# A PSUM tile for each of the seven products of a Strassen group

## Chip, core and metric

The kernel runs on one core of a Trainium2 chip. The metric is the time of one execution on the device in microseconds, 1038.79 as the median of three runs.

## What is computed

Four batches of eight heads attend over 576 positions of 64 elements: only scores within `tau` of a row's maximum count. The result, 2304 rows of 512, goes through four experts, weighted by the row's normalised domain probabilities.

```python
scores = scale * np.matmul(q, k.transpose(0, 1, 3, 2))
thresh = np.max(scores, axis=-1, keepdims=True) - tau
scores = np.where(scores >= thresh, scores, -1000000000.0)
scores = scores - np.max(scores, axis=-1, keepdims=True)
attn = np.exp(scores)
attn = attn / (np.sum(attn, axis=-1, keepdims=True) + 1e-09)
x = np.matmul(attn, v).transpose(0, 2, 1, 3).reshape(B * S, H * D)   # 2304 x 512
p = domain_probs / (domain_probs.sum(-1, keepdims=True) + 1e-09)
for e in range(E):                                                    # E = 4, F = 1024
    h = np.maximum(x @ w1[e], 0.0)
    out += p[:, e:e + 1] * (h @ w2[e])
```

## The kernel before

Every fp32 operand of a matmul of the experts is split into a high and a low fp16 half, and a product of two such operands is three matmuls. Experts 0 and 1 (`unit`, products at L1372, second layer at L1414) run between the steps of attention. Experts 2 and 3 (`unit7`, L1564) run after it and form their first layer by Strassen's scheme, seven products of half blocks in place of eight. The 2304 rows are dealt in five row sets (`GR`); a row set and an expert make a unit, ten units in all. Four sets have m = 256 columns, the set `(8,)` has m = 128.

A unit has four groups, k = 0 to 3, of seven products each. A product (`product`, six matmuls at L1627) sums into a PSUM region. Its readers bring it, scaled, into the SBUF tile `qt`: `copy` on ScalarE (L1657) for the first product of a group, `add` on VectorE (L1647) for the others; the product of S1 and T1 is added twice. `hidden` then makes a hidden block's high half on ScalarE (L1668) and its low half on VectorE (L1675). The second layer takes these in steps of three matmuls of 512 columns (`g2`, L1707), eight steps to a row tile, and `done` (L1725) adds the result to the accumulator. `run` (L1872) deals the steps of the unit before between the products of a unit.

PSUM holds eight banks of 512 fp32 columns. Attention has the pool `ma`, two tiles of a bank (`ET`, `rp` and `av` by use), and the tile `S` of three banks, taken once; the other three are the pool `mm` of the second layer. The Strassen products live in what is attention's: the first, third, fifth group of a unit's order and so on put their regions a, b, f, g at columns 0, 1280, 1024 and 256 of `S`; the groups between take `av` for a and g and `ET` for f and b. The seven products use a, b, f, g, a, b, g in this order. The maxima over the weight pairs (`w_pair`, L1451, with `all_max`) use spare columns of `S` (`am`, L350).

The order of all instructions comes from `Plan` (L22 to L216), a list scheduler: each operation has an engine, an estimated time, the values it reads and writes, the tiles of pools that it uses, and a priority. A tile can be had when a slot of its pool is free, and a slot is free `FREED` = 150 ns after the last user of the tile in it ends. The tiles of a pool are given in the order in which they are first named. The simulated order is then the order in which each engine's instructions are emitted, and the program's waits follow from who reads and writes which tile. Two things tie the stages: `later_kind` (L313) closes the pools of attention at the first tile of a later pool and opens those of `later` in their space, and `ends` holds every operation on a later pool's tile back until all of attention's products with v (`av_`) are done:

```python
ends = {i for i, o in enumerate(pl.ops) if o[2].__name__ == "av_"}
...
for o in pl.ops:
    if any(pl.kinds[x[0]][0] in later for x in o[4]):
        o[3].update(ends)
```

Of the kernel before, what the change touches and what calls it, by code (L numbers as in the profile page):

```python
# [9 lines left out]
FP32 = mybir.dt.float32  # L10
# [214 lines left out]
def topk_attention_moe_kernel(  # L225
# [43 lines left out]
    for name, n in (  # L269
# [3 lines left out]
        pools[name] = pool(name, n, on=first)  # L273
    pools["ma"] = pool("ma", 2, space=PSUM)

    s_all = pool("s", 1, space=PSUM).tile([128, 1536], FP32, name="S")
    pl.pool("b", 1)
# [32 lines left out]
    kind("acc2", "w", "w", [128, 2, DM], FP32)  # L310
    later = {"wp": 8, "xf": 1}

    def later_kind(name, p, shape, dt):  # L313
        def make():
            if p not in pools:
                first.close()
                for n, k in later.items():
                    pools[n] = ctx.enter_context(
                        tc.tile_pool(name=n, bufs=k, reuse_waits="tile")
                    )  # L320
            return pools[p].tile(shape, dt, tag=name, name=name)

        pl.kind(name, p, make)

    for name, n in later.items():
        pl.pool(name, n)
    later_kind("WP", "wp", [128, 2, 2816], FP16)
    later_kind("xf", "xf", [128, 4, 2, 256], FP32)
    kind("XT", "xt", "xt", [128, NK, 2, 128], FP16)
# [1121 lines left out]
    def w_pair(e, k, kd, prio):  # L1451
# [18 lines left out]
        )  # L1470
        au = am(("w", e, k))
        all_max(
# [88 lines left out]
    TX = {"T1": (0, 0), "T3": (0, 1), "T4": (1, 0), "T2": (1, 1)}  # L1561
    n_quad = 0

    def unit7(name, xs, m, tiles, u, last):  # L1564
        nonlocal n_quad
        e, top = PARTS[u][0], -1000.0
# [38 lines left out]
        for k in range(4):  # L1605
            P, qt, q = ("WP", (e, k)), ("qt", (u, name, k)), (u, name, k)
            if n_quad % 2:
                ps = [("av", ("q", q)), ("ET", ("q", q))]
                at = {"a": (0, 0), "g": (0, 256), "f": (1, 0), "b": (1, 256)}
            else:  # L1610
                ps = [("S", ("q", q))]
                at = {"a": (0, 0), "g": (0, 256), "f": (0, 1024), "b": (0, 1280)}
            n_quad += 1
            reg = lambda r, ps=ps, at=at: pl.t(*ps[at[r][0]])[:, at[r][1]:at[r][1] + m]
            pu = lambda r, ps=ps, at=at: ps[at[r][0]]
            wcs = wc[:, e, k:k + 1]
# [37 lines left out]
            def copy(reg=reg, pu=pu, qt=qt, q=q, tmp=tmp, wcs=wcs):  # L1654
                act(
                    m / 0.96 + 190,
                    lambda: nc.scalar.activation(  # L1657
                        out=tmp(0), in_=reg("a"), func=ACTF.Copy, scale=wcs
                    ),
                    [("p", "a") + q, ("wc", u)], [("t", 0) + q], use=[pu("a"), qt], prio=top,  # L1660
                )

            def hidden(i, j, f, qt=qt, q=q, tmp=tmp):
# [17 lines left out]

            first += [
                [(product, "a", "11", "11"), (copy,)],
                [(product, "b", "S2", "T2"), (add, "b", 0, 1)],
                [(product, "f", "S1", "T1"), (add, "f", 1, 2)],
                [(product, "g", "S3", "T3"), (add, "g", 1, 1), (add, "f", 1, 3),
                 (hidden, 3, 1, k + 4)],
                [(product, "a", "12", "21"), (add, "a", 0, 0), (hidden, 0, 0, k)],
                [(product, "b", "S4", "22"), (add, "b", 2, 2), (hidden, 2, 1, k)],
                [(product, "g", "22", "T4"), (add, "g", 1, 1), (hidden, 1, 0, k + 4)],  # L1690
            ]
# [80 lines left out]
    with tc.manual_schedule():  # L1772
# [59 lines left out]

        ends = {i for i, o in enumerate(pl.ops) if o[2].__name__ == "av_"}
        for u in range(NP1, len(PARTS)):
# [95 lines left out]
```

## Time and profile before

| | |
|---|---|
| runs | 1037.43, 1038.79, 1040.62 us (median 1038.79) |
| profiled execution | 1037.09 us, span 1035.3 us |
| TensorE busy | 978.8 us, 95% of the span |
| VectorE busy | 728.4 us, 70% |
| ScalarE busy | 558.8 us, 54% |
| GpSimd busy | 244.4 us, 24% |
| DMA | 95.99 MB, 93 GB/s on the mean |
| granted TensorE clock | 0.979 of full speed on the mean |

The engines are PE (TensorE; PEld is its weight load, which runs beside a matmul), DVE (VectorE), ACT (ScalarE), POOL (GpSimd) and SP (SyncE, which issues DMAs). Busy shares are averages over the whole span; attention and the experts 0 and 1 fill it up to about 664 us, the Strassen units the rest. A row of a timeline groups like instructions that follow each other: start, duration, engine, line, what is written and read, how many, and in brackets the idle time of the engine ahead of it and who ended it. The ends of matmuls are modelled, so a row's duration can reach past the next row's start.

### The profile page before, as it was taken

Reading aid. Unit: us, or ns where it says so; the run is one execution under the profiler, and the core shown is the slowest. Engines: PE = TensorE matmul, PEld = TensorE weight load, DVE = VectorE, ACT = ScalarE, POOL = GpSimd, SP = SyncE. Lnnn points to the kernel's source line nnn. Section 1 sums busy time; section 2 is a strip of 40 time slices with the busy share of each in tenths; the row PEclk is TensorE's granted clock in tenths of the full one; section 3 lists DMA queues with packets and bytes.
Section 4 is the critical chain, followed back from the end, with each engine's and each line's share of the span. In section 5 each row is a group of like instructions: output and inputs, shape, how many; then the busy total and the mean of one; then the engine's idle time right before and its main releaser. Section 6 shows DMA issues by size and latency. Waiting matters only on the chain.

```text
span 1035.3 us, 20228 instructions
## 1 busy us (share of the span) xinstructions
PE 978.8 (95%) x7538; PEld 626.3 (60%) x7538; DVE 728.4 (70%) x1788; ACT 558.8 (54%) x1177; POOL 244.4 (24%) x401
## 2 busy tenths in 40 slices
PE   6779978999989999999999999999999998999998
PEld 4465644666666556666556776766666666666663
DVE  3787778888778887888883636878665577655551
ACT  4788777766776768676765678533212132212120
POOL 1112526334344325433342323200000000000000
PEclk9889977999999999999999999999999999999999
DMA  6800477775689477865774224200200202001001
GB/s 173 246 11 12 101 159 172 127 129 96 145 148 215 89 120 154 157 139 107 134 114 100 82 95 141 82 21 22 72 31 22 72 11 72 11 1 52 31 1 41
DMA packets 243234, 95.99 MB, mean 93 GB/s; under 512 B 209600, under 2 KB 230080, under 8 KB 243136
## 3 DMA queue, kind: packets, MB, share of 16 engines
q1 hardware_dynamic: 243136, 94.71, 41.6%
q8 instruction: 59, 0.97, 0.4%
q14 instruction: 39, 0.32, 0.1%
HBM read 40.41 MB, written 14.16 MB: 53 GB/s over the span
## 4 chain that ended last, share of the span: by engine, by line
PE 76%; DMA 8%; DVE 6%; SPq 4%; ACT 3%; issue 2%; POOL 1%; DVEq 0%; ACTq 0%; POOLq 0%
PE mm L1707 16%; PE mm L1372 15%; PE mm L1414 15%; PE S L1627 9%; PE av L1256 5%; PE av L1627 4%; DMA PT<-E 4%; PE S L933 4%; PE ET L1627 3%; SPq L413 3%; DVE qt L1647 3%; DMA wraw<-in_moe_w_dram 2%; PE av L1265 1%; PE S L939 1%; DMA T<-R 1%
## 5 line engine op out<-in xcount | busy, mean ns | idle before, releaser
L1707 PE MATMUL mm<-WP,h 128*128 128x512 f16 x864 | 221.2, 379 | 0.0
L1414 PE MATMUL mm<-W,h 128*128 128x512 f16 x864 | 206.0, 380 | 0.7 <-ACT hr L1384 0.7
L1627 PEld LDWEIGHTS <-WP 128*128 128x128 f16 x1680 | 153.2, 97 | 86.0 <-issue 33.0
L1372 PEld LDWEIGHTS <-W 128*128 128x128 f16 x2016 | 175.6, 99 | 33.4 <-issue 5.2
L1372 PE MATMUL mm<-X,W 128*128 128x256 f16 (+1 forms) x1632 | 181.6, 268 | 4.7 <-ACT hr L1384 4.7
L1668 ACT ACTIVATE h<-qt 128x256 f16<-128x256 f32 (+1 forms) x160 | 61.8, 394 | 227.4 <-DVE qt L1647 227.3
L1399 POOL TENSOR_TENSOR h<-hr,h 128x256 f16<-128x256 f32 (+1 forms) x168 | 128.8, 774 | 121.2 <-ACT h L1392 93.8
L1015 ACT ACTIVATE E<-SS,sm 128x576 f32<-128x576 f32 x144 | 109.2, 768 | 39.6 <-DVE SS L992 25.3
L1024 DVE SCALAR_TENSOR_TENSOR E<-SS,sm,E 128x576 f32<-128x576 f32 x144 | 120.9, 850 | 12.6 <-ACT E L1015 8.1
L1414 PEld LDWEIGHTS <-h 128*128 128x128 f16 x864 | 81.3, 99 | 78.9 <-issue 2.2
L1007 POOL TENSOR_SCALAR sm<-sm,tau_p 128x1 f32<-128x1 f32 x144 | 69.3, 482 | 203.1 <-DVE SS L992 144.2
L1707 PEld LDWEIGHTS <-h 128*128 128x128 f16 x864 | 82.6, 98 | 55.6
L1149 DVE SCALAR_TENSOR_TENSOR E<-E,ri,E 128x576 f16<-128x576 f32 (+1 forms) x120 | 91.3, 785 | 14.0 <-ACT E L1143 13.3
L1647 DVE SCALAR_TENSOR_TENSOR qt<-S,wc,qt 128x256 f32<-128x256 f32 (+1 forms) x140 | 60.9, 454 | 56.4 <-PE S L1627 55.6
L1384 ACT ACTIVATE hr<-mm,wc 128x256 f32<-128x256 f32 (+1 forms) x168 | 73.1, 438 | 49.3 <-PE mm L1372 43.2
L992 DVE TENSOR_SCALAR_CACHE_REDUCE SS<-S,qc 128x576 f32<-128x576 f32 x108 | 86.2, 810 | 18.8 <-DMA PT<-E 8.4
L1143 ACT ACTIVATE E<-E,ri 128x576 f16<-128x576 f32 (+1 forms) x120 | 83.4, 723 | 24.1 <-DVE ri L1121 7.8
L1577 POOL TENSOR_SCALAR psc<-pnv,wpm 128x2 f32<-128x2 f32 (+1 forms) x20 | 7.4, 372 | 309.7 <-DVE acc L1725 270.6
L933 PE MATMUL S<-T 64*128 64x512 f16 (+3 forms) x440 | 75.3, 443 | 3.4 <-DVE SS L992 2.9
L1256 PE MATMUL av<-PT,V 128*64 128x320 f16 (+3 forms) x768 | 66.3, 317 | 8.2 <-DMA PT<-E 6.9
L1675 DVE SCALAR_TENSOR_TENSOR h<-qt,h 128x256 f16<-128x256 f32 (+1 forms) x160 | 60.2, 393 | 6.8 <-ACT h L1668 4.0
L1627 PE MATMUL S<-T,WP 128*128 128x256 f16 (+1 forms) x480 | 59.4, 261 | 4.1 <-DVE qt L1647 3.5
(146 smaller groups left out, 1167.2 us busy)
## 6 DMA issues: line engine op xcount, KB each, us to landing
wraw<-in_moe_w_dram SPq DMA_DIRECT2D x64, 256.0 KB, 4.1
part<-acc SPq DMA_DIRECT2D x18, 256.0 KB, 2.5
X<-x_dram SPq DMA_DIRECT2D x9, 512.0 KB, 3.9
acc<-part SPq DMA_DIRECT2D x18, 256.0 KB, 3.4
raw<-in_q_dram SPq DMA_DIRECT2D x32, 128.0 KB, 3.1
raw<-in_k_dram SPq DMA_DIRECT2D x32, 128.0 KB, 3.1
out_dram<-acc SPq DMA_DIRECT2D x16, 256.0 KB, 2.2
x_dram<-X SPq DMA_DIRECT2D x7, 512.0 KB, 4.0
```

What stands on the lines that cost most here:

```text
L933: nc.tensor.matmul(ps[:, 1024 * h:1024 * h + SM] if j < 4 else ps[rows(h), 0:SM], qm(h, a), km(h, c), start=(y == 0), stop=(y == last),)
L992: nc.vector.tensor_scalar(out=pl.t(*ssu)[:, S * h:S * h + S], in0=pl.t(*su)[:, 960 * h:960 * h + S], scalar1=qc[:, g, 2:3] if g >= NP * T3 ...
L1015: lambda h=h: nc.scalar.activation(out=pl.t(*eu)[:, S * h:S * h + S], in_=pl.t(*ssu)[:, S * h:S * h + S], func=ACTF.Exp, scale=-1.0, bias= ...
L1024: lambda h=h, col=col: nc.vector.scalar_tensor_tensor(out=pl.t(*eu)[:, S * h:S * h + S], in0=pl.t(*ssu)[:, S * h:S * h + S], scalar=pl.t(* ...
L1149: nc.vector.scalar_tensor_tensor(out=o, in0=e, scalar=pl.t(*ru)[:, h:h + 1], in1=hh, op0=ALU.mult, op1=ALU.subtract,)
L1256: nc.tensor.matmul(av[64 * h:64 * h + 64, 0:n], va(slice(0, 128), vp, 4 * h + c), ts(slice(0, 128), tp, 5 * h + c, 0, n), start=(c == 0 an ...
L1372: nc.tensor.matmul(ps[:, 0:n], w[:, wp, 0, c * 128:(c + 1) * 128], x[:, c, xp, c0:c0 + n], start=(i == 0), stop=(i == len(seq) - 1),)
L1399: lambda hu=hu, hru=hru: nc.gpsimd.tensor_tensor(out=pl.t(*hu)[:, 1, 0:n], in0=pl.t(*hru)[:, 0:n], in1=pl.t(*hu)[:, 0, 0:n], op=ALU.subtra ...
L1414: nc.tensor.matmul(ps, h[:, hp, 128 * i:128 * i + 128], w[:, wp, 1, :], start=(f == f0 and hp == 0 and wp == 0), stop=(f == f1 - 1 and hp ...
L1627: nc.tensor.matmul(reg(r), w[:, wp, o:o + 128], xb(b, c, xp), start=(n == 0), stop=(n == 5),)
L1647: lambda: nc.vector.scalar_tensor_tensor(out=tmp(o), in0=reg(r), scalar=wcs, in1=tmp(i), op0=ALU.mult, op1=ALU.add),
L1707: nc.tensor.matmul(ps, ht()[:, hp, 128 * i:128 * i + 128], w[:, wp, o:o + 512], start=(f == 0 and hp == 0 and wp == 0), stop=(f == NF - 1 ...
```

## The change

The pool `ma` and the tile `S` move to the group of pools that is closed when attention is done. In their place two later pools open: `q` with four tiles of one bank, `Q`, and `qa` with one, `QA`. Every product takes a `Q` tile of its own, named by unit, row set, group and number of the product (1, 6, 5, 7, 2, 3, 4 in place of a, b, f, g, a, b, g), and the maxima of the weight pairs take `QA`. `ends` becomes every operation that uses a pool which is given back, less those on which such an operation depends directly. Nothing else is changed: products, readers, halves, second layer and loads are the same.

```diff
-    pools["ma"] = pool("ma", 2, space=PSUM)
-
-    s_all = pool("s", 1, space=PSUM).tile([128, 1536], FP32, name="S")
+    pools["ma"] = pool("ma", 2, on=first, space=PSUM, side="right")
+
+    s_all = pool("s", 1, on=first, space=PSUM, side="right").tile([128, 1536], FP32, name="S")
...
-    later = {"wp": 8, "xf": 1}
+    later = {"wp": 8, "xf": 1, "q": 4, "qa": 1}
...
                 for n, k in later.items():
+                    on = {"space": PSUM, "side": "right"} if n[0] == "q" else {}
                     pools[n] = ctx.enter_context(
-                        tc.tile_pool(name=n, bufs=k, reuse_waits="tile")
+                        tc.tile_pool(name=n, bufs=k, reuse_waits="tile", **on)
                     )
...
+    later_kind("Q", "q", [128, 512], FP32)
+    later_kind("QA", "qa", [128, 512], FP32)
...
-        au = am(("w", e, k))
+        au = ("QA", (e, k))
...
-            if n_quad % 2:
-                ps = [("av", ("q", q)), ("ET", ("q", q))]
-                at = {"a": (0, 0), "g": (0, 256), "f": (1, 0), "b": (1, 256)}
-            else:
-                ps = [("S", ("q", q))]
-                at = {"a": (0, 0), "g": (0, 256), "f": (0, 1024), "b": (0, 1280)}
-            n_quad += 1
-            reg = lambda r, ps=ps, at=at: pl.t(*ps[at[r][0]])[:, at[r][1]:at[r][1] + m]
-            pu = lambda r, ps=ps, at=at: ps[at[r][0]]
+            pu = lambda r, q=q: ("Q", q + (r,))
+            reg = lambda r, pu=pu: pl.t(*pu(r))[:, 0:m]
...
             first += [
-                [(product, "a", "11", "11"), (copy,)],
-                [(product, "b", "S2", "T2"), (add, "b", 0, 1)],
-                [(product, "f", "S1", "T1"), (add, "f", 1, 2)],
-                [(product, "g", "S3", "T3"), (add, "g", 1, 1), (add, "f", 1, 3),
+                [(product, 1, "11", "11"), (copy,)],
+                [(product, 6, "S2", "T2"), (add, 6, 0, 1)],
+                [(product, 5, "S1", "T1"), (add, 5, 1, 2)],
+                [(product, 7, "S3", "T3"), (add, 7, 1, 1), (add, 5, 1, 3),
...
-        ends = {i for i, o in enumerate(pl.ops) if o[2].__name__ == "av_"}
+        gone = {"ma", "s", "am0", "am1", "tl", "tt", "vr", "v", "ss", "e", "pt", "rb", "x32", "rt", "r16", "sm"}
+        ends = {i for i, o in enumerate(pl.ops) if any(pl.kinds[x[0]][0] in gone for x in o[4])}
+        for i in sorted(ends):
+            ends -= pl.ops[i][3]
```

How the change moves instructions is shown at three places. Lines of the changed kernel from about L1627 on are six lower (its products are L1621, its second layer L1701, its adds L1641, its halves L1669). The number behind a tile's name tells one tile from another; `mm` is a second-layer tile, `X` and `T2` are rows and sums of rows, `WP` weights, `h` and `h2` hidden halves. A bracket names the engines on whose semaphores the instruction waits.

The first place is on TensorE, near the end of the program, where products alternate with second-layer steps; of each product and each step the first matmul stands here. Before:

```order
L1627 MATMUL S_127<-X_10231,WP_8602 128x256
...
L1707 MATMUL mm_12104<-WP_8115,h_12004 128x512
...
L1707 MATMUL mm_12191<-WP_7638,h2_11715 128x512
...
L1627 MATMUL S_127<-T2_11234,WP_8602 128x256 [waits Activation_49]
...
L1707 MATMUL mm_12191<-WP_7638,h2_11693 128x512
...
L1627 MATMUL S_127<-T2_11217,WP_8602 128x256 [waits DVE_49]
```

and now:

```order
L1621 MATMUL Q_12421<-X_10341,WP_8622 128x256 [waits DVE_49]
...
L1701 MATMUL mm_12343<-WP_8128,h_12237 128x512
...
L1701 MATMUL mm_12436<-WP_7651,h2_11930 128x512
...
L1621 MATMUL Q_12441<-T2_11415,WP_8622 128x256 [waits DVE_49]
...
L1701 MATMUL mm_12436<-WP_7651,h2_11906 128x512
...
L1621 MATMUL Q_12452<-T2_11396,WP_8622 128x256 [waits DVE_49]
```

The order is the same; each product has another tile, and its wait is for the reader that frees it. Over the program 274 of the 280 products have such a wait now, 203 before.

The second place is on TensorE where products of two groups follow each other with hardly a step between; again the first matmul of each product or step. Before:

```order
L1627 MATMUL S_127<-X_7227,WP_7880 128x256 [waits DVE_49]
...
L1627 MATMUL ET_8909<-X_7861,WP_7651 128x256 [waits DVE_49]
...
L1627 MATMUL S_127<-T2_8741,WP_7880 128x256 [waits Activation_49]
...
L1627 MATMUL S_127<-T2_8687,WP_7880 128x256
...
L1627 MATMUL av_8705<-T2_8741,WP_7651 128x256 [waits DVE_49]
...
L1627 MATMUL S_127<-T2_8687,WP_7880 128x256
...
L1627 MATMUL S_127<-X_7227,WP_7880 128x256
...
L1627 MATMUL av_9012<-X_7227,WP_8115 128x256 [waits DVE_49]
...
L1627 MATMUL ET_9023<-T2_8741,WP_8115 128x256 [waits DVE_49]
```

and now, a stretch of the same sort:

```order
L1621 MATMUL Q_9041<-T2_8668,WP_7897 128x256 [waits DVE_49]
...
L1621 MATMUL Q_9051<-X_7227,WP_7897 128x256 [waits Activation_49]
...
L1621 MATMUL Q_9060<-X_7870,WP_7897 128x256 [waits DVE_49]
...
L1701 MATMUL mm_8947<-WP_7662,h_9008 128x512
...
L1621 MATMUL Q_9075<-T2_8819,WP_7897 128x256 [waits DVE_49]
...
L1621 MATMUL Q_9084<-X_7227,WP_8128 128x256 [waits DVE_49]
...
L1621 MATMUL Q_9093<-T2_8819,WP_8128 128x256 [waits DVE_49]
...
L1621 MATMUL Q_9106<-T2_8668,WP_8128 128x256 [waits DVE_49]
...
L1621 MATMUL Q_9117<-T2_8668,WP_8128 128x256 [waits Activation_49]
```

Where `S` was taken in turn with `av` and `ET`, and two groups were in work by turns, there are now `Q` tiles one after another, and the products of a group stand closer together.

The third place is on VectorE in the first of those groups. Before:

```order
L1647 SCALAR_TENSOR_TENSOR qt_8805<-S_127,wc_174,qt_8805 128x256 x2
L1493 SCALAR_TENSOR_TENSOR WP_8602<-wraw_8196,wsc_175,WP_8602 128x1024
L1675 SCALAR_TENSOR_TENSOR h2_8894<-qt_8805,h2_8894 128x256
L1675 SCALAR_TENSOR_TENSOR h_8902<-qt_8805,h_8902 128x256
L1647 SCALAR_TENSOR_TENSOR qt_8805<-S_127,wc_174,qt_8805 128x256 x2
L1493 SCALAR_TENSOR_TENSOR WP_8602<-wraw_8498,wsc_175,WP_8602 128x768
L1675 SCALAR_TENSOR_TENSOR h2_8921<-qt_8805,h2_8921 128x256
L1675 SCALAR_TENSOR_TENSOR h_8932<-qt_8805,h_8932 128x256
L1439 SCALAR_TENSOR_TENSOR acc_8551<-mm_8828,psc_7966,acc_8551 128x512
L1647 SCALAR_TENSOR_TENSOR qt_8924<-ET_8909,wc_174,qt_8924 128x256
```

and now:

```order
L1641 SCALAR_TENSOR_TENSOR qt_8852<-Q_8885,wc_174,qt_8852 128x256
L1641 SCALAR_TENSOR_TENSOR qt_8852<-Q_8897,wc_174,qt_8852 128x256
L1442 SCALAR_TENSOR_TENSOR acc_8539<-mm_8823,psc_7977,acc_8539 128x512
L1641 SCALAR_TENSOR_TENSOR qt_8852<-Q_8872,wc_174,qt_8852 128x256
L1669 SCALAR_TENSOR_TENSOR h_8917<-qt_8852,h_8917 128x256
L1641 SCALAR_TENSOR_TENSOR qt_8852<-Q_8909,wc_174,qt_8852 128x256
L1669 SCALAR_TENSOR_TENSOR h2_8936<-qt_8852,h2_8936 128x256
L1641 SCALAR_TENSOR_TENSOR qt_8852<-Q_8919,wc_174,qt_8852 128x256
L1669 SCALAR_TENSOR_TENSOR h2_8951<-qt_8852,h2_8951 128x256
L1641 SCALAR_TENSOR_TENSOR qt_8954<-Q_8938,wc_174,qt_8954 128x256
```

Adds (L1647, now L1641) of two tiles stood together; now each comes singly, with the low halves (L1675, now L1669) and other work between them.

## Rows read from the trace of the kernel before

**Rows 1.** Page, part 1: busy time, share of the span, instructions of each engine.

```profile
PE 978.8 (95%) x7538; PEld 626.3 (60%) x7538; DVE 728.4 (70%) x1788; ACT 558.8 (54%) x1177; POOL 244.4 (24%) x401
```

**Rows 2.** Windows 150 to 200 and 664.12 to 1009.31: window, length, busy (instructions) by engine, clock, DMA share, GB/s.

```profile
150.00:200.00 50.00, 42.47 (x303) 24.37 (x304) 42.51 (x100) 34.97 (x77) 20.23 (x33) 0.83 0.77 159
664.12:1009.31 345.19, 335.24 (x2382) 218.19 (x2380) 222.82 (x522) 88.23 (x209) 6.82 (x18) 1.00 0.11 37
```

**Rows 3.** Waits of PE, 664.12 to 1009.31: total us, times, longest.

```profile
PE S L1627 <- DVE qt L1647: 7.9, 21, 0.7
PE ET L1627 <- DVE qt L1647: 0.7, 1, 0.7
PE av L1627 <- DVE qt L1647: 0.6, 1, 0.6
PE S L1627 <- ACT qt L1657: 0.5, 1, 0.5
```

**Rows 4.** Windows of L1627, then L1707: window, length, PE and PEld busy (instructions).

```profile
664.12:1009.31 345.19, 194.29 (x1616) 146.84 (x1613) 1.00 0.11 37
...
664.12:1009.31 345.19, 199.19 (x763) 72.83 (x764) 1.00 0.11 37
```

**Rows 5.** Chain that ended last: start of the step, its us, engine, tile, line.

```profile
545.61 10.48 PE mm L1372 x96
...
1009.31 22.03 PE mm L1707 x102
```

**Rows 6.** Timeline 646 to 648, PE: start, us, engine, line, operation.

```profile
646.20 1.50 PE L1372 MATMUL mm<-XT,W 128*128 128x128 f16 x24
```

**Rows 7.** Timeline 759 to 770, a group on S.

```profile
759.27 0.82 PE L1627 MATMUL S<-X,WP 128*128 128x256 f16 x6
...
759.92 1.46 PE L1707 MATMUL mm<-WP,h 128*128 128x512 f16 x6
...
760.18 0.48 ACT L1657 ACTIVATE qt<-S,wc 128x256 f32<-128x256 f32 x1 [0.43 <-PE S L1627]
...
761.22 0.82 PE L1627 MATMUL S<-T,WP 128*128 128x256 f16 x6
...
762.15 0.48 DVE L1647 SCALAR_TENSOR_TENSOR qt<-S,wc,qt 128x256 f32<-128x256 f32 x1 [0.63 <-PE S L1627]
...
762.69 0.82 PE L1627 MATMUL S<-T,WP 128*128 128x256 f16 x6
...
766.32 0.88 DVE L1647 SCALAR_TENSOR_TENSOR qt<-S,wc,qt 128x256 f32<-128x256 f32 x2 [0.91 <-PE S L1627]
...
767.25 0.81 PE L1627 MATMUL S<-X,WP 128*128 128x256 f16 x6 [0.32 <-DVE qt L1647]
...
769.94 0.82 PE L1627 MATMUL av<-X,WP 128*128 128x256 f16 x6
```

**Rows 8.** Timeline 770 to 780, the group on av and ET.

```profile
772.83 0.48 DVE L1647 SCALAR_TENSOR_TENSOR qt<-ET,wc,qt 128x256 f32<-128x256 f32 x1 [0.57 <-PE ET L1627]
...
773.36 0.81 PE L1627 MATMUL ET<-T,WP 128*128 128x256 f16 x6
...
779.96 0.27 PE L1627 MATMUL S<-X,WP 128*128 128x256 f16 x1
```

**Rows 9.** Timeline 658 to 675, products without steps between.

```profile
658.17 0.81 PE L1627 MATMUL S<-X,WP 128*128 128x256 f16 x6 [0.45 <-DVE qt L1647]
...
659.43 1.28 DVE L1493 SCALAR_TENSOR_TENSOR WP<-wraw,wsc,WP 128x1024 f16<-128x1024 f32 x1
...
671.32 0.81 PE L1627 MATMUL S<-X,WP 128*128 128x256 f16 x6 [0.33 <-DVE qt L1647]
...
672.17 1.66 DVE L1647 SCALAR_TENSOR_TENSOR qt<-S,wc,qt 128x256 f32<-128x256 f32 x4 [0.91 <-PE S L1627]
...
673.88 0.82 PE L1627 MATMUL S<-T,WP 128*128 128x256 f16 x6 [0.44 <-DVE qt L1647]
```

**Rows 10.** Windows 833 to 886, all engines (columns as in rows 2).

```profile
833.00:886.00 53.00, 49.55 (x421) 34.55 (x420) 40.91 (x106) 17.35 (x43) 1.50 (x4) 1.00 0.14 41
```

More of the change, by code (lines that the diff above doesn't have):

```diff
@@ L1561, in topk_attention_moe_kernel @@
     TX = {"T1": (0, 0), "T3": (0, 1), "T4": (1, 0), "T2": (1, 1)}
-    n_quad = 0
     def unit7(name, xs, m, tiles, u, last):
-        nonlocal n_quad
         e, top = PARTS[u][0], -1000.0
@@ L1657, in copy @@
                     lambda: nc.scalar.activation(
-                        out=tmp(0), in_=reg("a"), func=ACTF.Copy, scale=wcs
+                        out=tmp(0), in_=reg(1), func=ACTF.Copy, scale=wcs
                     ),
-                    [("p", "a") + q, ("wc", u)], [("t", 0) + q], use=[pu("a"), qt], prio=top,
+                    [("p", 1) + q, ("wc", u)], [("t", 0) + q], use=[pu(1), qt], prio=top,
                 )
@@ L1682, in unit7 @@
             first += [
-                [(product, "a", "11", "11"), (copy,)],
-                [(product, "b", "S2", "T2"), (add, "b", 0, 1)],
-                [(product, "f", "S1", "T1"), (add, "f", 1, 2)],
-                [(product, "g", "S3", "T3"), (add, "g", 1, 1), (add, "f", 1, 3),
+                [(product, 1, "11", "11"), (copy,)],
+                [(product, 6, "S2", "T2"), (add, 6, 0, 1)],
+                [(product, 5, "S1", "T1"), (add, 5, 1, 2)],
+                [(product, 7, "S3", "T3"), (add, 7, 1, 1), (add, 5, 1, 3),
                  (hidden, 3, 1, k + 4)],
-                [(product, "a", "12", "21"), (add, "a", 0, 0), (hidden, 0, 0, k)],
-                [(product, "b", "S4", "22"), (add, "b", 2, 2), (hidden, 2, 1, k)],
-                [(product, "g", "22", "T4"), (add, "g", 1, 1), (hidden, 1, 0, k + 4)],
+                [(product, 2, "12", "21"), (add, 2, 0, 0), (hidden, 0, 0, k)],
+                [(product, 3, "S4", "22"), (add, 3, 2, 2), (hidden, 2, 1, k)],
+                [(product, 4, "22", "T4"), (add, 4, 1, 1), (hidden, 1, 0, k + 4)],
             ]
```

## The prediction

> **What bounds the kernel now.** I begin with the busy shares of the page. TensorE is busy 978.8 of 1035.3 us, VectorE 728.4 [rows 1], so time can be won only where TensorE stands still or works slowly. The change touches the part after attention, so I cut out the stage from 664.12 us, a little after the last product of experts 0 and 1, to 1009.31 us, where the last run of second-layer matmuls begins. In it TensorE's granted clock is 1.00 throughout, that is 2.4 GHz [rows 2]: nothing is to be won at the clock. What is left are the waits. In this stage every wait of TensorE that the trace names is of one kind: a product's first matmul waits for the VectorE or ScalarE instruction that reads an earlier product out of the same PSUM tile [rows 3]. They are only 9.7 us in 24 waits, 22 of them on tile S. No wait on a load, on weights or on the second layer stands there.
>
> That list understates the loss. The trace draws a product's six matmuls 0.82 us long and the next instruction's start 0.65 us after the first one's [rows 7], since the end of a matmul is modelled. So about 0.16 us of every wait hides under the tail of the matmul ahead, and a wait shorter than that does not show. I therefore count the work and take it from the elapsed time. Prices, from stretches with nothing between: 96 matmuls of 256 columns in 10.48 us, 0.1092 each; 102 of 512 columns in 22.03 us, 0.216 each [rows 5]; 24 of 128 columns in 1.50 us, drawn with the longer tail, so about 0.056 each [rows 6]. The stage holds 1616 matmuls of the products (1280 of 256 columns and 336 of 128, the row set with m = 128) and 763 of the second layer [rows 4]:
>
> 1280 x 0.1092 + 336 x 0.056 + 763 x 0.216 = 139.8 + 18.8 + 164.8 = 323.4 us; three other matmuls of the stage are some 0.4 more. Elapsed are 345.2, so **21.4 us** are stalls. The group that ends just before 664 has about 1.0 us more of them (the product at 658.17 waits a visible 0.45 [rows 9], with the 0.16 that hides 0.61, and three others lose 0.1 to 0.2 each), so 22.4 in all.
>
> **Where they are.** In 740 to 833 and 886 to 1009 us products alternate with second-layer steps: 22 groups, 18 of them wide. A wide group is 7 products and 8 steps: 42 x 0.1092 + 24 x 0.216 = 9.77 us. A group on S takes 769.94 - 759.27 = 10.67 [rows 7], so it loses 0.90; the next one, on the two tiles av and ET, takes 779.96 - 769.94 = 10.02 [rows 7, 8] and loses 0.25. The rows tell why. On S the product at 761.22 is read by the add at 762.15, which lasts 0.48, and the next product, in another region of S, starts at 762.69, 0.06 later [rows 7]: each product waits for the reader of the one just before. The pitch is 1.39 us where the work is 0.655 + 0.648 = 1.30, a loss of 0.09 each time, and where two adds run together (766.32, 0.88) the next starts at 767.25, some 0.48 late. On av and ET a product follows the other tile mostly, and only the third waits like that (772.83 and 773.36 [rows 8]). Nine groups of each sort give 9 x 0.90 + 9 x 0.25 = 10.4, the four narrow ones, taken at half the time for a wait more or less, some 0.5: **11 us**. The other 11.4 us lie in the stretches where products follow each other with no step between, 664 to 740 and 833 to 886.
>
> **The change, part by part.** (a) The seven tiles of their own. The schedule keeps the order of the work in the alternating stretches; in the run stretches it no longer takes products of two groups by turns, but one group after the other. Each product waits for the reader of one 2 to 7 products earlier, mostly 4, since the pool has four slots. In alternating stretches four products back is four pitches, 5.2 us; the reader needs 0.93 us from the product's start to its own start, 0.48 to run and 0.06 for the signal, 1.5 us [rows 7]. Even the product that is read twice, with a second add one pitch of 1.30 us later, comes free in about 2.8 us. So those 11 us go entirely. What is late next there: nothing that the trace shows; the second-layer matmuls have no wait in the stage [rows 3].
>
> (b) In the run stretches four products back are 4 x 0.655 = 2.6 us against the same 1.5, so VectorE may fall behind by 1.1 us before TensorE waits. It does fall behind at times: an instruction that makes weight halves takes 1.28 us between two adds [rows 9], and it is queued ahead of the reader. Bounds: all 11.4 us vanish, or all stay. I take **2 us left**, nearer the first end, for two reasons. The waits there are those of a tile shared by regions, as elsewhere (671.32 and 673.88, both on S [rows 9]). And VectorE there waits for TensorE as much as the reverse: the four adds at 672.17 follow an idle time of 0.91 us, ended by a product [rows 9]. In 833 to 886 VectorE is busy 40.9 of 53.0 us [rows 10]; shortened by its share of the 11.4 us (53 of the 129 us of both run stretches, 4.7), the stretch still has 48 us for them.
>
> (c) More waits stand in the code: in the schedule 274 of the 280 products have one on their first matmul, 203 before. Behind it on TensorE stand the second-layer steps, which a late reader would hold up too. A wait already met costs nothing: the product at 761.22 waits for ScalarE's copy, done at 760.66, and starts where the six matmuls from 759.92 on end, 759.92 + 6 x 0.216 = 761.22 [rows 7]. Ends: 0, and 71 x 0.06 = 4 us by the signal's time; I take 0 by that row.
>
> (d) The maxima of weight pairs use one tile in place of two, and attention's tiles are given back before the first product. Queues at that place keep their order but for one VectorE instruction (L1532) moved behind two evictions, and the weights' DMA loads on SP stand as before. Weights are ready before products need them in the stage (no such wait in [rows 3]); so 0, with an end of 2 us lost if a first product comes later. The cover is the rest of expert 1's work, which TensorE can take first.
>
> (e) The last run of 102 second-layer matmuls, 22.03 us [rows 5], does not change, nor does all before 650 us.
>
> **Sum.** The profiled execution took 1037.1 us (span 1035.3), 1.7 under the median of 1038.8. 1037.1 - 22.4 + 2 = 1016.7; with the median as base 1018.4. I say **1017.5 us**. Ends: all stalls gone, 1014.7, or a little lower as the execution's own spread goes; run stretches as they are, 1037.1 - 11 = 1026, and 2 more for (d), 1028.
>
> **The clock weighed.** It is 1.00 in the whole stage with its 24 waits of up to 0.7 us, and 0.83 on the mean in 150 to 200 us, where TensorE is idle 7.5 of 50 us [rows 2, 3]. The change takes idle time away, so by these rows the clock stays, and the sum with it. A rule speaks against this: the Trainium skill, "TensorE: Matmul & The Clock Gate", section "A second HAM failure mode: psum-queue depth-cycling", says that a kernel whose groups of matmuls cycle through PSUM banks can idle for a moment between groups so often that the clock swings between its levels. By it the changed stage, with four banks in turn, would lose clock, to the time of rival D; the trace of before, which already goes round three tiles, does not agree.
>
> **The rivals.**
> (A) The run stretches keep their loss: VectorE, not the tile, is the limit there, and four slots only move the wait. For it: VectorE at 77% in 833 to 886 [rows 10], and the 1.28 us instruction. Against it: VectorE's idle of 0.91 before the adds. Time 1026. Chance 0.18.
> (B) Slower: four slots are too few. S held four regions and av and ET four more, eight products of two groups, where now four are in flight in all. A tile is held from the first matmul to the end of its reader; if the readers came late by more than 1.1 us in the run stretches or 3.7 in the others, each group would lose a wait. One of 0.65 us (a whole product) in each of 40 groups is 26 us, more than the 22.4 won: 1041. Against it: readers wait for products, not products for late readers (idle 0.91 us before the adds at 766.32 and 672.17 [rows 7, 9]). It decides from about 0.56 us per group on. Chance 0.03.
> (C) The wait moves on to the second layer: products run ahead, and steps wait for the hidden halves that VectorE and ScalarE make. No step waits now [rows 3]. Gain between 0 and 10, 1027 to 1037; chance 0.05, of it 0.02 within 0.3%.
> (D) The turn through four tiles brings short idle times at every product, and with them the clock falls: at the 0.83 of [rows 2] the 323.8 us of work in the stage become 390, against 345 now, and the time about 1037 + 45 = 1082. Against it: clock 1.00 with waits as they are. Chance 0.01. (This is the Trainium skill's rule just named.)
> (E) It does not do what it says: the pool still orders the tiles so that a product waits for the reader just ahead. The schedule's waits, on readers four back, speak against it. 1037 to 1039; chance 0.03.
>
> **Numbers.** The forecast has 0.70. The range, 1013 to 1028, holds it and A, and leaves out B to E and a little of both ends. About 0.3%, 3.1 us, is what a measurement of this kernel can tell from no change. Faster by more: 0.70 + 0.18 + 0.03 = 0.91; within it 0.02 + 0.03 = 0.05; slower 0.03 + 0.01 = 0.04.
>
> **What would show it.** Right: in the alternating stretch a group of 9.77 us on the mean of two neighbours, where there are 10.67 and 10.02; the list of TensorE's waits on readers down from 9.7 to about 1 us; the last run of 102 beginning near 989 instead of 1009.31; stage stalls of 2 to 3 us by the same count. Wrong: waits on VectorE near 5 us or more in the run stretches (A); product waits in every group, alternating ones too (B); idle before the second-layer matmuls (C); a clock under 1.00 after 664 us (D); S-like pitches of 1.39 (E).

## The result and the profile after

| | before | after |
|---|---|---|
| runs | 1037.13 to 1040.62 us, median 1038.11 | 1011.52 to 1014.45 us, median 1013.25 |
| ratio, 95% interval | | 0.9756, 0.9732 to 0.9779 |
| profiled execution (span) | 1037.09 (1035.3) us | 1012.9 (1011.1) us |
| TensorE idle from 650 us to the last run of 102 | 10.4 us | 0.0 us |
| stalls by the count | 23.5 us | 0.3 us |

The change makes the kernel faster by 24.9 us. The count in the last row is the prediction's, taken matmul by matmul: from the second product of the first group to the last run of 102 second-layer matmuls, each start is compared with the next one's, less the price of the matmul (0.1092 us for 256 columns, 0.216 for 512, 0.056 for 128), and what goes beyond the price is added up. With the starts that come a little early taken off it is 22.8 us before and 0.0 after. The count is good to about 0.3 us. It also sees the delays that hide under a modelled end.

First the busy line of the changed kernel's page and, from its list of the costliest groups (busy time and mean of one ahead of the second bar, idle time ahead of the group behind it), the second layer, the adds and two forms of the products:

```profile
PE 963.3 (95%) x7538; PEld 625.3 (62%) x7538; DVE 729.0 (72%) x1788; ACT 558.1 (55%) x1177; POOL 240.8 (24%) x401
...
L1701 PE MATMUL mm<-WP,h 128*128 128x512 f16 x864 | 218.3, 379 | 0.0
...
L1641 DVE SCALAR_TENSOR_TENSOR qt<-Q,wc,qt 128x256 f32<-128x256 f32 (+1 forms) x280 | 123.2, 455 | 75.6 <-PE Q L1621 72.0
...
L1621 PE MATMUL Q<-T,WP 128*128 128x256 f16 (+1 forms) x960 | 116.3, 262 | 0.0
...
L1621 PE MATMUL Q<-X,WP 128*128 128x256 f16 (+1 forms) x720 | 88.2, 262 | 0.0
```

The products stand with an idle time of 0.0, where the kernel before had waits of 9.7 us on readers [rows 3]. The adds, which each wait for their product, are what waits now, on an engine that has time for it. The same stretch by windows (columns as in [rows 2]):

```profile
650.00:985.10 335.10, 335.10 (x2466) 226.85 (x2464) 234.67 (x544) 95.70 (x225) 9.76 (x22) 1.00 0.12 38
```

TensorE is busy for 335.10 of 335.10 us, with the clock at 1.00. By its content the stretch costs just that: 1338 x 0.1092 + 336 x 0.056 for its 1674 matmuls of products, and 787 x 0.216 for those of 512 columns, are 334.9 us. In the timeline of an alternating stretch, TensorE's products and one add:

```profile
741.04 0.82 PE L1621 MATMUL Q<-X,WP 128*128 128x256 f16 x6
...
744.29 0.82 PE L1621 MATMUL Q<-T,WP 128*128 128x256 f16 x6
...
745.15 0.48 DVE L1641 SCALAR_TENSOR_TENSOR qt<-Q,wc,qt 128x256 f32<-128x256 f32 x1 [0.18 <-PE Q L1621]
...
745.59 0.82 PE L1621 MATMUL Q<-T,WP 128*128 128x256 f16 x6
...
750.80 0.82 PE L1621 MATMUL Q<-X,WP 128*128 128x256 f16 x6
...
760.57 0.82 PE L1621 MATMUL Q<-X,WP 128*128 128x256 f16 x6
```

Two groups in a row take 750.80 - 741.04 = 9.76 and 760.57 - 750.80 = 9.77 us, the forecast pitch, where a group on S took 10.67 and the next one 10.02 [rows 7, 8]. The product at 745.59 starts 0.44 after an add began that still runs: it writes another tile. The last step in the chain of waits answers to the second of [rows 5]:

```profile
985.10 22.03 PE mm L1701 x102
```

It is as long as before and begins 24.2 us earlier.

### The profile page after: what moved, and what is told of

Same layout as the page of the kernel before. It is cut to its first block, busy times and chain, and to the rows that moved or that the text cites. A ratio compares the mean times of both kernels' runs of the same rounds, so it can differ in the third digit from the quotient of the medians.

```text
span 1011.1 us, 20235 instructions
## 1 busy us (share of the span) xinstructions
PE 963.3 (95%) x7538; PEld 625.3 (62%) x7538; DVE 729.0 (72%) x1788; ACT 558.1 (55%) x1177; POOL 240.8 (24%) x401
## 4 chain that ended last, share of the span: by engine, by line
PE 78%; DMA 8%; DVE 5%; SPq 4%; ACT 3%; issue 2%; POOL 1%; DVEq 0%; ACTq 0%; POOLq 0%
PE mm L1701 18%; PE Q L1621 16%; PE mm L1417 15%; PE mm L1375 14%; PE av L1259 5%; PE S L936 4%; DMA PT<-E 4%; SPq L416 3%; DMA wraw<-in_moe_w_dram 3%; PE av L1268 1%; PE S L942 1%; PE ET L1047 1%; DVE SS L995 1%; ACT W L843 1%; DVE E L1152 1%
## 5 line engine op out<-in xcount | busy, mean ns | idle before, releaser
L1701 PE MATMUL mm<-WP,h 128*128 128x512 f16 x864 | 218.3, 379 | 0.0
L1621 PEld LDWEIGHTS <-WP 128*128 128x128 f16 x1680 | 153.5, 98 | 58.1
L1641 DVE SCALAR_TENSOR_TENSOR qt<-Q,wc,qt 128x256 f32<-128x256 f32 (+1 forms) x280 | 123.2, 455 | 75.6 <-PE Q L1621 72.0
L1402 POOL TENSOR_TENSOR h<-hr,h 128x256 f16<-128x256 f32 (+1 forms) x168 | 125.8, 757 | 121.7 <-ACT h L1395 85.6
L1701 PEld LDWEIGHTS <-h 128*128 128x128 f16 x864 | 82.8, 98 | 59.6
L1621 PE MATMUL Q<-T,WP 128*128 128x256 f16 (+1 forms) x960 | 116.3, 262 | 0.0
L1621 PE MATMUL Q<-X,WP 128*128 128x256 f16 (+1 forms) x720 | 88.2, 262 | 0.0
```

Of the source, the lines that this page charges most:

```text
L1402: lambda hu=hu, hru=hru: nc.gpsimd.tensor_tensor(out=pl.t(*hu)[:, 1, 0:n], in0=pl.t(*hru)[:, 0:n], in1=pl.t(*hu)[:, 0, 0:n], op=ALU.subtra ...
L1621: nc.tensor.matmul(reg(r), w[:, wp, o:o + 128], xb(b, c, xp), start=(n == 0), stop=(n == 5),)
L1641: lambda: nc.vector.scalar_tensor_tensor(out=tmp(o), in0=reg(r), scalar=wcs, in1=tmp(i), op0=ALU.mult, op1=ALU.add),
L1701: nc.tensor.matmul(ps, ht()[:, hp, 128 * i:128 * i + 128], w[:, wp, o:o + 512], start=(f == 0 and hp == 0 and wp == 0), stop=(f == NF - 1 ...
```

## The experiments

Each kernel was timed on one chip together with the kernel before, whose median lay between 1036.4 and 1037.7 us in these sets; the ratio is to that one. "Stalls" is the count above, on each kernel's own profile.

| kernel | median, us | ratio to before, 95% | stalls, us |
|---|---|---|---|
| e_undo2: regions again | 1038.1 | 0.9985 to 1.0024 | 22.5 |
| e_mown: own tiles for av/ET groups | 1034.0 | 0.9953 to 0.9985 | 19.8 |
| e_sown: own tiles for S groups | 1019.2 | 0.9797 to 0.9887 | 5.4 |
| e_pair: two products to a tile | 1018.4 | 0.9796 to 0.9844 | 3.8 |
| e_q2: two tiles | 1018.2 | 0.9804 to 0.9845 | 6.0 |
| e_q3: three tiles | 1017.1 | 0.9781 to 0.9838 | 1.5 |
| e_onetile: one tile of four banks | 1107.9 | 1.0655 to 1.0701 | 93.7 |
| e_twice: low halves made twice | 1025.4 | 0.9868 to 0.9909 | 9.8 |
| e_ends: old rule for the start | 1016.6 | 0.9749 to 0.9845 | 0.3 |
| e_again: the change once more | 1015.5 | 0.9779 to 0.9831 | 0.3 |

**Undoing the regions alone.** The first try, of which the new pool of one tile `QS` of two banks is left out here:

```diff
-            pu = lambda r, q=q: ("Q", q + (r,))
-            reg = lambda r, pu=pu: pl.t(*pu(r))[:, 0:m]
+            if n_quad % 2:
+                ps, at = [("Q", q + (0,)), ("Q", q + (1,))], {1: (0, 0), 2: (0, 0), 7: (0, 256), 4: (0, 256), 5: (1, 0), 6: (1, 256), 3: (1, 256)}
+            else:
+                ps, at = [("QS", q)], {1: (0, 0), 2: (0, 0), 7: (0, 256), 4: (0, 256), 5: (0, 512), 6: (0, 768), 3: (0, 768)}
+            n_quad += 1
+            pu = lambda r, ps=ps, at=at: ps[at[r][0]]
+            reg = lambda r, pu=pu, at=at: pl.t(*pu(r))[:, at[r][1]:at[r][1] + m]
```

> The changed kernel with its moved pools, its own tile for the weight maxima and its rule for the start, but the products back in regions: groups by turns in one tile of two banks (a, g, f, b side by side, one wait for all) and in two tiles of one bank, as before. Theory (the gain is the wait of a product for the reader of another region of its tile, nothing else): the gain goes back, 1036 to 1040 us, TensorE's waits on readers near 10 us again, a group in the one tile 10.67 and in the two tiles 10.02 us. Rival (the moved pools and the rule for the start bring part of it): 1025 to 1035, with shorter time already ahead of the first group. Rival (they bring all): 1013.

It took 1035.3 us with 19.4 us of stalls. Its schedule could let a region's second product overtake the readers of the first, so that part of the sums is mixed; its time is not used. The second try adds the missing order by naming a product's value, for the schedule, after its region (in `add` and `copy` likewise):

```diff
+            pk = lambda r, at=at, q=q: ('p', at[r]) + q
...
-                    [("p", r) + q], use=[pu(r), P] + xu, prio=1000 + n_moe,
...
+                    [pk(r)], use=[pu(r), P] + xu, prio=1000 + n_moe,
```

> The edit of e_undo again, with one thing added: the schedule is told, as in the kernel before, that a region's second product of a group comes after the readers of its first. Theory (all of the gain is the wait for the reader of another region of the tile): 1034 to 1040 us, and counted against the prices of the matmuls 20 to 24 us of stalls ahead of products, as before (23.5). Rival (moved pools, own tile for the maxima and the rule for the start bring part of the gain): stalls as before, but 2 us or more less elsewhere, so under 1034.

1038.1 us, and the waits of TensorE (us in total, times, longest) are much like those of [rows 3], 10.0 us in all:

```profile
PE QS L1630 <- DVE qt L1650: 8.4, 21, 0.7
PE QS L1630 <- ACT qt L1660: 1.0, 2, 0.6
PE Q L1630 <- DVE qt L1650: 0.6, 1, 0.6
```

So the moved pools, the own tile of the maxima and the rule for the start bring nothing that can be measured, the interval of the ratio being some 2 us to either side: the tiles bring all that can be.

**Half the groups.** In e_sown the groups that were on S take two tiles of their own, in e_mown the others do; the rest stays as in e_undo2.

> Only the groups that were on S get own tiles (two, of a bank each); the others stay on two tiles with two regions each. Theory: the loss of a group on S (0.90 where steps lie between) falls to at most 0.25 of another cause (two tiles in turn), that of the others stays (0.25): stalls of 4 to 9 us, 1018 to 1024 us. Rival (what matters is the number of regions in flight, which stays the same or falls): 20 us or more, 1033 to 1040.

> Only the groups that were on av and ET get own tiles (two); the others stay in four regions of one tile. Theory: the loss of the groups in the one tile stays, 0.90 each where steps lie between and more where products follow each other: stalls of 12 to 20 us, 1026 to 1035 us; with e_sown the two gains add up to about the whole (23 us). Rival (either half of the groups gives most of the gain, since a group on own tiles runs while the other waits): under 1024.

Waits of TensorE in e_sown, then in e_mown:

```profile
PE Q L1630 <- DVE qt L1650: 0.6, 3, 0.2
PE QH L1630 <- DVE qt L1650: 0.3, 1, 0.3
```

```profile
PE QS L1630 <- DVE qt L1650: 9.4, 21, 0.8
PE QS L1630 <- ACT qt L1660: 1.2, 3, 0.6
```

Both came out as the theory has it. Of the 22.5 us of e_undo2, e_sown takes 17.1 away and e_mown 2.7, together 19.8: the tile with four regions carried most of the loss. Counted by the tile that the waiting product writes, e_undo2 loses 18.5 us on QS and 3.9 on Q. In e_sown 0.5 are left on the own tiles QH and 4.7 on Q, in e_mown 0.2 on QH and 19.6 on QS: own tiles take nearly all of their own groups' loss away, and the groups left in regions lose a microsecond or so more than they did. Why they do was not tried.

**Tile or bank.** e_onetile leaves each of the four regions in a bank to itself, in the same four banks, but as one tile (a product's value is again named after its region, as in e_undo2, which is left out here):

```diff
-    later = {"wp": 8, "xf": 1, "q": 4, "qa": 1}
+    later = {"wp": 8, "xf": 1, "q": 1, "qa": 1}
...
-    later_kind("Q", "q", [128, 512], FP32)
+    later_kind("Q", "q", [128, 2048], FP32)
...
-            pu = lambda r, q=q: ("Q", q + (r,))
-            reg = lambda r, pu=pu: pl.t(*pu(r))[:, 0:m]
+            ps, at = [("Q", q)], {1: (0, 0), 2: (0, 0), 6: (0, 512), 3: (0, 512), 5: (0, 1024), 7: (0, 1536), 4: (0, 1536)}
+            pu = lambda r, ps=ps, at=at: ps[at[r][0]]
...
+            reg = lambda r, pu=pu, at=at: pl.t(*pu(r))[:, at[r][1]:at[r][1] + m]
```

> The same four banks as in the change, but as one tile of four banks; each of the four regions has a bank to itself, and the schedule is told of a region's second product. Theory (waits follow the tile, not the bank): every product waits for the reader of the one just ahead, 0.09 us each where steps lie between and 0.17 to 0.5 where two adds meet, some 0.9 a wide group, 18 us and more over the alternating stretches, and up to 0.85 a product where products follow each other; 30 to 80 us of stalls, 1040 to 1100 us. Rival (waits follow the bank, and S lost only because two regions shared a bank): no wait but for a region's own reader, stalls of 0 to 6 us, 1013 to 1021 us.

1107.9 us, above the theory's upper end and far from the rival's. The two largest of its waits on TensorE, and then a stretch of its timeline where products follow each other:

```profile
PE Q L1623 <- DVE qt L1643: 54.4, 100, 1.8
PE Q L1623 <- ACT qt L1653: 12.0, 21, 0.6
```

```profile
717.21 0.82 PE L1623 MATMUL Q<-T,WP 128*128 128x256 f16 x6 [0.65 <-DVE qt L1643]
...
718.06 0.48 DVE L1643 SCALAR_TENSOR_TENSOR qt<-Q,wc,qt 128x256 f32<-128x256 f32 x1 [0.91 <-PE Q L1623]
718.60 0.81 PE L1623 MATMUL Q<-X,WP 128*128 128x256 f16 x6 [0.57 <-DVE qt L1643]
...
719.45 0.48 DVE L1643 SCALAR_TENSOR_TENSOR qt<-Q,wc,qt 128x256 f32<-128x256 f32 x1 [0.91 <-PE Q L1623]
719.99 0.81 PE L1623 MATMUL Q<-X,WP 128*128 128x256 f16 x6 [0.57 <-DVE qt L1643]
```

The product at 718.60 starts when the add that began at 718.06 is done, and the next add waits for that product: TensorE and VectorE work by turns, 1.39 us a product for 0.655 of work. The banks are those of the change; what differs is what counts as one tile, and with it the schedule, which has one slot to deal. What my upper end of 80 us of stalls left out was not taken apart; with one tile the next group also has to wait for the last reader of this one.

e_pair keeps four tiles and lets two successive products share one:

```diff
-            pu = lambda r, q=q: ("Q", q + (r,))
-            reg = lambda r, pu=pu: pl.t(*pu(r))[:, 0:m]
+            pu = lambda r, q=q: ("Q", q + ({1: 0, 6: 0, 5: 1, 7: 1, 2: 2, 3: 2, 4: 3}[r],))
+            reg = lambda r, pu=pu: pl.t(*pu(r))[:, (0, 256)[r in (6, 7, 3)]:][:, 0:m]
```

> Four tiles as in the change, but two successive products share one, in two regions of it (1 and 6, 5 and 7, 2 and 3; 4 alone). Theory (a product waits for the readers of its whole tile): the second of each pair waits for the reader of the first, just ahead: 0.1 to 0.5 us each where steps lie between, 6 to 10 us over the stage, and up to 0.85 us for each of three where products follow each other, which the schedule does not know of, 20 to 36 us: 1035 to 1060 us, slower than the kernel before or about as slow. Rival (regions wait for their own readers alone, and the gain is from more regions): 1011 to 1016.

The wait is there, but the size was off by far: 1018.4 us. Where steps lie between, the timeline shows the pitch of 1.39 us once more, from the third product of a group to its partner, and 1.30 after it:

```profile
745.78 0.82 PE L1621 MATMUL Q<-T,WP 128*128 128x256 f16 x6
...
746.63 0.48 DVE L1641 SCALAR_TENSOR_TENSOR qt<-Q,wc,qt 128x256 f32<-128x256 f32 x1 [0.18 <-PE Q L1621]
...
747.17 0.81 PE L1621 MATMUL Q<-T,WP 128*128 128x256 f16 x6
...
748.47 0.82 PE L1621 MATMUL Q<-X,WP 128*128 128x256 f16 x6
```

Where products follow each other there is next to no stall. There the two products of a pair stand ahead of the reader of the first, and then it is the reader that waits, as the later of the two on the tile. ScalarE's copy shows it, first in e_pair and then in the changed kernel:

```profile
664.82 0.82 PE L1621 MATMUL Q<-X,WP 128*128 128x256 f16 x6
665.47 0.82 PE L1621 MATMUL Q<-T,WP 128*128 128x256 f16 x6
...
666.33 0.47 ACT L1651 ACTIVATE qt<-Q,wc 128x256 f32<-128x256 f32 x1 [4.45 <-PE Q L1621]
```

```profile
665.58 0.82 PE L1621 MATMUL Q<-X,WP 128*128 128x256 f16 x6
...
666.24 2.13 PE L1621 MATMUL Q<-T,WP 128*128 128x256 f16 x18
666.44 0.47 ACT L1651 ACTIVATE qt<-Q,wc 128x256 f32<-128x256 f32 x1 [1.14 <-PE Q L1621]
```

In the changed kernel the copy starts 0.86 us after its own product (665.58), with the next one at work; in e_pair it starts 1.51 after its own (664.82) and 0.86 after the partner (665.47). So the wait falls to whichever comes second in the order of the program, and when that is a reader, ScalarE or VectorE pays, which has time. My expectation had it fall on the product every time.

**How many tiles.** The only edit is the 4 of `"q": 4`, to 3 and to 2.

> Three tiles in place of four, each product still with its own. Theory (a tile is needed for about 1.5 us from a product's start, 2.8 when it is read twice): three products back are 3.9 us where steps lie between, so no wait there; 1.96 us where products follow each other, so waits wherever VectorE is 0.5 us late: 1013 to 1020 us, all of the loss in the stretches without steps. Rival (the number of tiles in flight is what the gain rests on, VectorE being late everywhere): over 1025, with waits in the alternating stretches too.

> Two tiles in place of four. Theory: two products back are 2.6 us where steps lie between, so only the product that is read twice (2.8 us) costs 0.2 or so a group, 5 us over 22 groups; where products follow each other two back are 1.3 us against 1.5, some 0.2 to 0.9 a product, 10 to 25 us: 1028 to 1043 us. Rival (slots hardly matter once each product has a tile): 1013 to 1018.

Three tiles came out as expected, 1.5 us of stalls. Two tiles did not: 10 to 25 us were expected where products follow each other, and all stalls together are 6.0; 1018.2 us lies 10 under the theory's range and at the upper end of the rival's. The order is likely to explain it: runs of three or more products with no step between are 6 in e_q2 and 16 after the change, and pairs 70 in place of 9. TensorE of e_q2:

```profile
679.64 0.82 PE L1621 MATMUL Q<-X,WP 128*128 128x256 f16 x6
680.30 0.81 PE L1701 MATMUL mm<-WP,h 128*128 128x512 f16 x3
681.03 1.47 PE L1621 MATMUL Q<-T,WP 128*128 128x256 f16 x12
682.33 1.46 PE L1701 MATMUL mm<-WP,h 128*128 128x512 f16 x6
```

The schedule knows the number of tiles and puts steps between the pairs, so that readers have time. That this is the cause was argued and not tried: no run holds the order fixed.

**How much room VectorE has.** In e_twice each low half is made twice, which the schedule is not told:

```diff
-                    lambda: nc.vector.scalar_tensor_tensor(
+                    lambda: [nc.vector.scalar_tensor_tensor(
...
-                    ),
+                    ) for _ in range(2)],
```

> The change, with each low half made twice on VectorE (0.41 us more, four times a group, 160 times in all; the schedule is not told). Theory (a tile is back after about 1.5 us of the four products it lasts, so VectorE has room to be later): where steps lie between, a group takes VectorE 6.4 of 9.8 us, no stall; where products follow each other 6.4 against 5.2 us, so TensorE waits there for up to 1.2 us in each of some 14 groups: 5 to 17 us of stalls, 1019 to 1031 us. Rival A as forecast (VectorE is the limit in those stretches already): all 66 us of added work beyond the room show there, over 1035. Rival (VectorE has room everywhere, as it lags and catches up): 1013 to 1017.

The busy line of its page, and its waits on TensorE:

```profile
PE 966.7 (95%) x7538; PEld 625.7 (61%) x7538; DVE 783.2 (77%) x1948; ACT 558.7 (55%) x1177; POOL 242.7 (24%) x401
```

```profile
PE Q L1621 <- DVE qt L1641: 5.4, 11, 0.9
PE Q L1621 <- DVE WP L1496: 0.4, 1, 0.4
```

VectorE is busy 54 us longer and the stalls grow by 9.5, all of it in the run stretches, as the theory had it; 1025.4 us. So VectorE is not the limit after the change, but in the run stretches it is near: about a sixth of the work added to it came back as time.

**The rule for the start, and the whole once more.** e_ends takes the old rule for `ends` with the new tiles:

```diff
-        ends = {i for i, o in enumerate(pl.ops) if any(pl.kinds[x[0]][0] in gone for x in o[4])}
-        for i in sorted(ends):
-            ends -= pl.ops[i][3]
+        ends = {i for i, o in enumerate(pl.ops) if o[2].__name__ == "av_"}
```

> The change with the old rule for the start: all operations on later tiles wait in the schedule for attention's products with v alone. Theory (this rule is worth nothing): stalls as in the change, 0.3 us, 1012 to 1017 us. Rival (the new rule brings a microsecond or two by starting weights or the first product in a better place): 1016 to 1020 us, with the first products or the maxima of the weight pairs waiting.

> The changed kernel once more, unaltered, timed in more rounds and with a second profile. In the first profile the stage has 0.3 us of stalls by the count, against 23.5 before, while the medians lie 24.9 apart; 2.5 us of the two profiles' distance were there at 540 us already, where both run the same instructions. Theory (stalls are the gain, the rest is how an execution's loads fall in attention): ratio to before 0.976 to 0.979, a distance of 22 to 25 us, and at 540 us this profile may lie on either side of that of before. Rival (the change also shortens attention by 2 us through the place of its PSUM tiles): 24 to 27 us, and again 2 us ahead at 540.

e_ends has the stalls of the change, 0.3 us; its runs reach from 1009.6 to 1021.3, too wide to see a microsecond in, and their median lies in the ranges of both. e_again gives 1015.5 us, 22.1 under the kernel before of its set, with the same 0.3 us of stalls. The distance is in the expected range, the ratio (the middle of its interval is 0.9805) a little above 0.979; the rival's 24 to 27 us did not come.

## Why the prediction was right and wrong

The direction, the place and the mechanism were right; the size was too small: 21.3 us forecast (1038.8 to 1017.5), 24.9 measured, 22.1 in the second measurement. The time of 1013.25 lies at the very end of the range (1013 to 1028): two of the four runs, 1011.52 and 1012.90 us, are below it, and by the ratio, 0.9756 of 1038.11, it is 1012.8. The term of the sum that was mis-sized is (b), 2 us left where nothing is left; and the lower end allowed too little for what attention takes from one execution to the next.

- **What bounds the kernel, the count of 22.4 us: right.** Matmul by matmul it is 23.5, or 22.8 net, and no other limit showed up behind it. The prices held: the stretch after the change takes what they say.
- **(a) Alternating stretches, 11 us: right.** By the count they held 12.3 us and the rest 11.2. Groups take 9.77 us now, and e_sown and e_mown show the loss on S to be several times that on av and ET. Two readings of rows were inexact. The products at 761.22 and 762.69 stand 1.47 us apart, a loss of 0.17; the 1.39 is the pitch of the next one. And on av and ET not only the third product waits; the fifth loses 0.09 as well (776.05 - 774.66 = 1.39). In the kernel before:

```profile
764.08 0.82 PE L1627 MATMUL S<-T,WP 128*128 128x256 f16 x6
...
774.66 0.82 PE L1627 MATMUL av<-T,WP 128*128 128x256 f16 x6
...
776.05 0.81 PE L1627 MATMUL av<-X,WP 128*128 128x256 f16 x6
```

  The sum of 11 us went by whole groups and does not hang on these.
- **(b) Run stretches, 2 us left: this step failed.** Nothing is left: the count finds no stall of a product there, and the last run of 102 begins at 985.10 us, not near 989 (2.5 us of that distance arise in attention). The step held that a late reader, behind an instruction of 1.28 us, would sometimes stop TensorE, with room of 1.1 us. The adds are late there at times, in the changed kernel for one:

```profile
661.01 1.47 PE L1621 MATMUL Q<-T,WP 128*128 128x256 f16 x12
...
662.27 1.01 DVE L1496 SCALAR_TENSOR_TENSOR WP<-wraw,wsc,WP 128x768 f16<-128x768 f32 x1
662.32 1.47 PE L1621 MATMUL Q<-X,WP 128*128 128x256 f16 x12
663.19 1.65 DVE L1641 SCALAR_TENSOR_TENSOR qt<-Q,wc,qt 128x256 f32<-128x256 f32 x4
663.63 1.46 PE L1701 MATMUL mm<-WP,h 128*128 128x512 f16 x6
...
664.93 0.82 PE L1621 MATMUL Q<-T,WP 128*128 128x256 f16 x6
```

  The second product of the first row could be read from about 662.5 on (661.01 + 0.655 + 0.86) and is read at 663.19, behind an instruction for weight halves; no product waits. The four tiles and the steps between take it up, even three tiles leave only 1.5 us, and with 54 us more work for VectorE there are 9.8. Rival A is out by the same runs. How much of the gain in these stretches the tiles bring and how much the new order of the products was not separated; in the alternating stretches the order stays, and there it is the tiles.
- **(c) More waits: 0, right.** All remaining excess is 0.3 us.
- **(d) Start and maxima: 0 taken, up to 2 allowed; it was about 1.** In the changed kernel one maximum of a weight pair waits on TensorE, at 582 us, for VectorE's sum, where the kernel before has no such wait (waits of TensorE, 500 to 660 us):

```profile
PE QA L445 <- DVE st L1469: 0.8, 1, 0.8
```

  With the 0.16 that hides this is 1.0 us given back, the only cost of the change that shows. It comes and goes: e_again has one of this length at 604 us, e_twice, whose schedule is that of the change, has none, and neither has e_ends with the old rule. VectorE's sum waits there for ScalarE, and ScalarE for a load of weights.
- **(e) The tail: right**, 22.03 us as before.
- **The sum.** 23.2 us of stalls gone (23.5 less 0.3), less 1.0, is 22.2, where the forecast had 22.4 less 2, 20.4. The second measurement's 22.1 agrees with it. So do the profiles: from one matmul near 540 us, ahead of which nothing differs in TensorE's work, to the last run of 102 the kernel before takes 469.0 us, the changed one 447.3 and 447.5 in its two profiles, 21.8 and 21.5 less, and e_undo2 468.9. The rest of the first measurement's 24.9 is, as far as is known, what attention takes from one execution to the next: in the first profile 2.5 us of the distance are there at 540 us already; in the profile of e_again it is 0.8. That the forecast of 21.3 comes so near to 22.2 is in part luck, as its base, between profile and median, added 0.9 us to the 20.4. The lower end of the range had next to nothing for the spread.
- **Rivals.** B (too few tiles): three tiles cost 1.5 and two 6.0 us of stalls, so four are far from the point where it decides. C: the second layer's idle time is 0.0. E: the pitch of 1.39 is gone. D, the clock: it is 1.00 after the change, and also in e_onetile, where TensorE is idle 68 of 427 us in more than 120 short waits between groups of matmuls:

```profile
650.05:1077.14 427.09, 358.73 (x2455) 225.24 (x2454) 235.83 (x541) 95.60 (x222) 12.45 (x21) 1.00 0.09 30
```

  The Trainium skill, "TensorE: Matmul & The Clock Gate", section "A second HAM failure mode: psum-queue depth-cycling", tells of a kernel that goes through PSUM banks in turn and whose clock swings between its levels as TensorE idles for moments between groups of matmuls; no run of this case shows it, and the 1.00 of e_onetile speaks against it here.

## What to carry to other kernels

A tile is what the program waits for here: regions of one tile that different products write and different readers read are one resource, also when they lie in banks of their own. Ask of each region which instruction comes second in program order, since that one waits, and give the engine that must not stop tiles of its own; two or three did most of it here. Count work by start-to-start prices, as what hides under the modelled end of a matmul, short waits and a part of each longer one, does not show in a list of waits: here it was more than half of the loss (9.7 us listed of 21.4 [rows 3]).

## What the runs showed that was not expected

Executions of identical instructions differ by several microseconds in attention. At the same matmul near 540 us the profiles of e_ends and e_q3 are 6.8 and 2.5 us later than that of the kernel before, that of the change 2.5 earlier. One place where this arises, by windows over the same instructions, in the kernel before and in the changed one (columns as in [rows 2]):

```profile
440.94:453.37 12.43, 10.23 (x78) 5.65 (x76) 8.54 (x20) 7.01 (x13) 0.85 (x4) 0.86 0.77 163
```

```profile
440.68:450.75 10.07, 8.62 (x77) 4.87 (x76) 7.68 (x19) 6.36 (x12) 0.79 (x3) 1.00 0.78 197
```

and TensorE's first row behind the load there, in the same order:

```profile
445.22 2.48 PE L1256 MATMUL av<-PT,V 128*64 128x320 f16 x21 [2.20 <-DMA PT<-E]
```

```profile
444.17 1.65 PE L1259 MATMUL av<-PT,V 128*64 128x320 f16 x21 [1.45 <-DMA PT<-E]
```

TensorE waits for the transfer of PT 2.20 us in place of 1.45, and the granted clock of the stretch, in the mean, is 0.86 in place of 1.00 (of 2.4 GHz): 21 matmuls take 2.48 us in place of 1.65, and the stretch 12.4 in place of 10.1. So a longer wait for a transfer is followed here by a larger loss at the clock; whether the one causes the other was not tried.
